# Three token tiles instead of one pass the feed-forward layer in fp32 from unsplit weights, and every later block holds one tile

## The chip, the cores and the metric

The kernel runs on one core of a Trainium2 chip. The metric is the device time of one execution in microseconds (us): the median of three runs is 649.31, the lowest 649.01, the highest 651.72. One execution was also recorded by the profiler.

## What is computed

Attention with rotary position embedding, then a feed-forward layer (FFN) on its output. The weights arrive as float64.

```python
q_rot, k_rot = (rotate(q), rotate(k))            # q, k, v: 4 x 8 heads x 576 x 64
scores = scale * np.matmul(q_rot, k_rot.transpose(0, 1, 3, 2))
scores = scores - np.max(scores, axis=-1, keepdims=True)
attn = np.exp(scores)
attn = attn / (np.sum(attn, axis=-1, keepdims=True) + 1e-09)
x = np.matmul(attn, v)                           # heads joined: x is 2304 x 512
h = x @ w_in                                     # 512 x 2048
relu6 = np.clip(h + 3.0, 0.0, 6.0)
g = h * relu6 / 6.0
out = (g @ w_out).astype(np.float32)             # 2048 x 512
```

## The kernel before, in words

The 2304 tokens are 18 tiles of 128 rows (`NT`), and tile t has 8 heads, so there are 144 attention steps. Tile 0 is done in fp32 throughout (`attention_first`, `emit_first`). The 136 steps of tiles 1 to 17 work on split numbers: an fp32 matrix is cut into a high and a low fp16 half, and a product is the sum of three fp16 products (high-high, high-low, low-high).

One fp16 attention step (`attention`) is: four matmuls for the scores S (L610; L613 where a tile belongs to two batches, as tiles 4 and 13 do), a scaling with the row maximum on VectorE (L657), the exponential on ScalarE (L659), the high half on ScalarE (L666), the low half on VectorE (L670), a DMA transposition, and 14 matmuls with V (L628). S has two buffers, which are free again after L670.

The weights are loaded in 16 pieces, 8 of w_in and 8 of w_out. Each is decoded from float64 (`decode_w`; L530, L543 or L545, L551, and L557 on VectorE), bounded (L247 or L249), and later split: `split_w_steps` makes the high half by ScalarE, GpSimd or VectorE (L292, L296, L294) and the low half by VectorE (L304, 128x1024). The split halves overwrite the unsplit weights, so a piece is split only when the tiles that need it unsplit have used it (`used_h` and `used`).

The FFN goes block by block (`BLK`). Blocks 0 to 3 hold one tile each, blocks 4 to 10 two tiles each. `ffn_h` makes x @ w_in: for each of 16 slices of 128 hidden columns it runs 4 fp32 matmuls (block 0, L893) or 12 fp16 matmuls (L906), whose moving side has 128 columns for one tile and 256 for two. `gate` makes g on ScalarE and VectorE and, for fp16 blocks, splits it into halves. `ffn_o` makes g @ w_out: per tile 16 fp32 matmuls of 512 columns (block 0, L973) or 48 fp16 ones (L977). `NF` and `NH` give how many blocks go in fp32. For an fp16 block `emit_x` divides the attention output by the row sums, splits it and transposes it by DMA.

The order of the work is not written by hand. The class `Emission` plays the program through with assumed durations and a table of priorities (`CFG`), and the instructions are recorded in the order in which this play starts them; on the chip each engine then runs its own list in that order, waiting where it must. Rules in the play: attention step i is let in by `attn_ready` (among other things: no more than `lead` = 32 steps ahead of the FFN's units, and from step 16 on only when the first w_out piece is split). `keep_clock` puts idle matmuls (L1031, result unused) into TensorE's gaps until tile 2's attention is done.

Of the kernel before, what the change touches and what calls it, by code (L numbers as in the profile page):

```python
# [185 lines left out]
def attention_ffn(ctx: ExitStack, tc, q, k, v, w_in, w_out, rope, ident, out):  # L186
# [610 lines left out]
    def emit_first():  # L797
# [19 lines left out]
        free("av")  # L817
        x_done.add(0)

    def emit_x(t):  # L820
# [20 lines left out]
        yield from scaled("xh", 512, x16[:, 0:512], x)
        e = yield "Xxl", {"P": 1.16, "d": 0.68}
        ENG[e].tensor_tensor(out=x16[:, 512:1024], in0=x, in1=x16[:, 0:512], op=ALU.subtract)  # L843
        if n == 0:
            yield "C", lambda: ((j < 3 or (j - 3) in h_done)
                                and (j % 3 == 0 or min([wdone["i"]] + used_h) >= 5 + j % 3))
            nn = 128 * len(BLK[j])
            xT_t[j] = xT_mem[j % 3][:, 0:8 * nn].rearrange("p (c n) -> p c n", c=8)
# [11 lines left out]
    def scales(j):  # L860

        for sums, kind, x in ((osc, "i", GAM * 2.0 ** -28), (out_sc, "o", 2.0 ** -16 / 6.0)):
            yield "C", lambda: kind in p2w
# [8 lines left out]

    def ffn_h(js):

        for j, ts in ((j, BLK[j]) for j in js):
# [4 lines left out]
            xT = xT_t[j]  # L880
            for u in range(4 * len(ts)):
                yield "R", "g"
                pooled = g_free.pop()
                yield "R", "h"
                h = psum.tile([128, nm, N], F32, tag="h", bufs=2, name="h")
                for i in range(nm):
                    m = u * nm + i
# [10 lines left out]
                    yield "C", lambda: wdone["i"] >= p  # L898
                    n = 0
                    for c in range(4):  # L900
                        if j < len(BLK) - 1:
                            yield "E", 0.67 / nm
                        elif c == 0:
                            yield "E", 4 * 0.65 / nm
# [233 lines left out]
```

## Time and profile before

| | |
|---|---|
| median of the runs | 649.31 us |
| profiled execution, first to last instruction | 647.6 us |
| TensorE matmuls busy | 579.7 us (90%) |
| VectorE busy | 457.2 us (71%) |
| ScalarE busy | 386.1 us (60%) |
| GpSimd busy | 309.1 us (48%) |

The profile's page gives busy times for the whole execution, but the stages differ. In the first 64 us weights are loaded and decoded and tile 0 is in attention; from some 200 us on TensorE is busy nearly throughout; between them lies a stretch in which TensorE has gaps and VectorE hardly any. The span of the profiled execution is 1.7 us under the median of the runs. Busy time of matmuls includes a modelled tail of some 0.16 us after each group, in which the next group already runs.

### The profile page before, as it was taken

The page shows a single profiled execution, that of the slowest core. Times are in us where ns is not written, and L with a number is a line of the kernel's source. Part 1 is how long each engine was busy: PE and PEld are TensorE (multiplying, and loading weights), DVE is VectorE, ACT ScalarE, POOL GpSimd, SP SyncE. Part 2 cuts the span into 40 slices and gives each one's busy share as a digit, 9 for nine tenths or more (in the row PEclk, how much of TensorE's full clock was granted, in tenths as well). Part 3 has the DMA queues.
Part 4 walks back from the last instruction along what each step waited for, and adds up shares of the span by engine and source line. Part 5 has one row for each costly group of instructions (what it writes and reads, how often), then busy time and mean ns, then how long its engine had stood idle before and what let it go on. Part 6 is the DMA issues. An engine that isn't in the chain of part 4 may idle for free.

```text
span 647.6 us, 15265 instructions
## 1 busy us (share of the span) xinstructions
PE 579.7 (90%) x6024; PEld 421.3 (65%) x6024; DVE 457.2 (71%) x860; ACT 386.1 (60%) x716; POOL 309.1 (48%) x347
## 2 busy tenths in 40 slices
PE   2488889478889999998998999999999999999997
PEld 1367755366666776675675767776677677667756
DVE  6999979999976896588697787775777656312430
ACT  4875998745855676577576756665567556322111
POOL 3573545597425596545399452562445425133000
PEclk9989889989989999999999999999999999999999
DMA  9995494986969988999998999778699775410000
GB/s 309 319 321 138 143 262 96 198 139 108 199 129 165 212 158 142 182 157 187 213 151 138 171 225 184 122 151 143 114 161 178 111 142 98 84 33 17 1 17 33
DMA packets 252439, 97.98 MB, mean 151 GB/s; under 512 B 235856, under 2 KB 236240, under 8 KB 252368
## 3 DMA queue, kind: packets, MB, share of 16 engines
q1 hardware_dynamic: 252368, 97.01, 73.4%
q8 instruction: 47, 0.77, 0.5%
q14 instruction: 24, 0.20, 0.1%
HBM read 31.97 MB, written 4.72 MB: 57 GB/s over the span
## 4 chain that ended last, share of the span: by engine, by line
PE 62%; DVE 12%; POOL 9%; DMA 8%; issue 6%; ACT 3%; SPq 0%; DVEq 0%; POOLq 0%; ACTq 0%
PE o L977 22%; PE h L906 20%; DMA PT<-P 7%; PE av L628 7%; PE S L610 6%; POOL ropeA L279 2%; PE o L973 2%; DVE P L670 2%; POOL kst L284 2%; DVE S L657 2%; POOL kst L282 2%; PE S L699 1%; PE S L613 1%; PE h L893 1%; DVE tg L930 1%
## 5 line engine op out<-in xcount | busy, mean ns | idle before, releaser
L906 PEld LDWEIGHTS <-wi_st 128*128 128x128 f16 x1920 | 164.8, 99 | 52.6 <-issue 3.0
L977 PE MATMUL o<-wo_st,g 128*128 128x512 f16 (+1 forms) x738 | 184.2, 367 | 3.7 <-ACT wo_st L1001 1.6
L906 PE MATMUL h<-wi_st 128*128 128x256 f16 (+1 forms) x1344 | 160.1, 259 | 0.8 <-DVE tg L930 0.7
L659 ACT ACTIVATE S<-S,mx 128x576 f32<-128x576 f32 x136 | 97.0, 713 | 101.9 <-DVE S L657 100.2
L657 DVE TENSOR_SCALAR_CACHE_REDUCE S<-S,sig 128x576 f32<-128x576 f32 x136 | 109.6, 819 | 33.2 <-PE S L610 26.4
L670 DVE SCALAR_TENSOR_TENSOR P<-S,P 128x576 f16<-128x576 f32 x136 | 100.9, 752 | 31.9 <-ACT P L666 31.5
L977 PEld LDWEIGHTS <-g 128*128 128x128 f16 x738 | 69.1, 98 | 44.4 <-POOL g L941 6.2
L296 POOL TENSOR_SCALAR g<-tg 128x512 f16<-128x512 f32 x37 | 23.6, 638 | 153.8 <-DVE tg L930 144.2
L930 DVE SCALAR_TENSOR_TENSOR tg<-tg,h 128x512 f32<-128x512 f32 x68 | 46.4, 683 | 70.8 <-ACT tg L923 70.8
L923 ACT ACTIVATE tg<-h,g,block_sc 128x512 f32<-128x512 f32 x68 | 52.7, 775 | 71.8 <-PE h L906 70.7
L628 PEld LDWEIGHTS <-PT 128*128 128x128 f16 (+1 forms) x2128 | 72.8, 102 | 34.7 <-DMA PT<-P 17.7
L610 PE MATMUL S<-kT,qT 128*128 128x288 f16 x480 | 77.0, 289 | 14.0 <-DVE P L670 13.9
L666 ACT ACTIVATE P<-S 128x576 f16<-128x576 f32 x135 | 85.5, 647 | 1.8
L628 PE MATMUL av<-vA,PT 128*128 128x64 f16 (+1 forms) x1520 | 63.8, 196 | 13.3 <-DMA PT<-P 12.3
L906 PE MATMUL h<-xTa,wi_st 128*128 128x256 f16 (+1 forms) x576 | 68.4, 255 | 0.0
L610 PEld LDWEIGHTS <-qT 128*128 128x128 f16 x480 | 44.1, 99 | 33.4 <-DVE P L670 13.8
L941 POOL TENSOR_TENSOR g<-tg,g 128x512 f16<-128x512 f32 x51 | 59.2, 1161 | 8.2 <-ACT g L292 5.3
L628 PE MATMUL av<-vB,PT 128*128 128x64 f16 (+1 forms) x608 | 38.9, 195 | 0.0
L977 PE MATMUL o<-wo_st 128*128 128x512 f16 (+1 forms) x126 | 32.7, 369 | 0.6 <-POOL wo_st L941 0.6
L279 POOL TENSOR_TENSOR ropeA<-kst,rope_sb 128x512 f32<-128x512 f32 (+1 forms) x16 | 20.9, 1307 | 13.3 <-DMA kst<-in_k 12.6
L843 POOL TENSOR_TENSOR x<-x,x 128x512 f16<-128x512 f32 x15 | 18.2, 1215 | 18.0 <-ACT x L292 18.0
L659 ACT ACTIVATION_READ_ACCUMULATOR S<-S,mx 128x1 f32 x136 | 26.6, 195 | 0.0
(157 smaller groups left out, 794.6 us busy)
## 6 DMA issues: line engine op xcount, KB each, us to landing
raw<-in_w_in SPq DMA_DIRECT2D x16, 512.0 KB, 7.4
raw<-in_w_out SPq DMA_DIRECT2D x16, 512.0 KB, 4.7
qraw<-in_q SPq DMA_DIRECT2D x18, 256.0 KB, 3.3
kst<-in_k SPq DMA_DIRECT2D x16, 256.0 KB, 4.0
out<-wo_st SPq DMA_DIRECT2D x16, 256.0 KB, 2.5
vst<-in_v SPq DMA_DIRECT2D x15, 256.0 KB, 4.8
PT<-P SPq DMA_TRANSPOSE x136, 3.4
vB<-vA SPq DMA_DIRECT2D x8, 256.0 KB, 3.6
```

Of the source, the lines that this page charges most:

```text
L279: ENG[e].tensor_tensor(out=v4(ta), in0=x4[:, :, ::-1, :], in1=sinb.to_broadcast([n, 8, 2, 32]), op=ALU.mult)
L610: PE.matmul(out=S[:, j, 0:288], lhsT=qT_t[t][:, o, h, :], rhs=kT_t[b0][:, h, ks], **st)
L628: PE.matmul(out=av[r0:r1, h, :], lhsT=PT[:, blk, r0:r1], rhs=rhs, start=(n == 0), stop=(n == len(terms) - 1))
L657: DVE.tensor_scalar(out=E, in0=E, scalar1=sig_t[t], scalar2=3.0e38, op0=ALU.mult, op1=ALU.min, accum_out=mx)
L659: ACT.activation(out=E, in_=E, func=ACTF.Exp, scale=-1.0, bias=mx, accum_out=sum_t[t][:, h:h + 1])
L666: ACT.activation(out=hi, in_=E, func=ACTF.Copy, scale=ES)
L670: DVE.scalar_tensor_tensor(out=lo, in0=E, scalar=ES, in1=hi, op0=ALU.mult, op1=ALU.subtract)
L906: PE.matmul(out=h[:, i, :], lhsT=wi_h(p, wl)[:, 256 * c + f0:256 * c + f0 + 128], rhs=xT[:, 4 * xl + c, :], start=(n == 0), stop=(n == 11))
L923: ACT.activation(out=tg, in_=hf, func=ACTF.Relu, scale=osc[j], bias=g3)
L930: DVE.scalar_tensor_tensor(out=whole if j < NF else tg, in0=tg, scalar=6.0 * GAM, in1=hf, op0=ALU.min, op1=ALU.mult)
L941: ENG[e].tensor_tensor(out=gf[:, 1], in0=tg, in1=gf[:, 0], op=ALU.subtract)
L977: PE.matmul(out=os[n][0][:, to], lhsT=g[:, gl, mm % nm, 128 * n:128 * n + 128], rhs=wo_h(mm, wl)[:, cs], start=(mm == 0 and gl == 0 and wl ...
```

## The change

`NF` and `NH` go from 1 to 3: tiles 0, 1 and 2 go through both products in fp32 with unsplit weights, and the pieces are split only behind tile 2. Every block holds one tile, so there are 18 blocks, and all fp16 matmuls of the first product have 128 moving columns. For tiles 1 and 2 a new `emit_x32` divides, transposes x on TensorE in fp32 and copies it. The first three tiles' attention no longer waits for w_out's splits. The first product's generator gets a priority of its own (`CFG["h"]`, 6.0), and the other numbers of `CFG` are new: `lead` goes from 32 to 18, `kvs` from 1 to 0 (the second batch's K and V are started when all 16 pieces are decoded, instead of when w_out's third piece is split), `vpos` from 0 to 3.

```diff
-BLK = [[0]] + [[t] for t in range(1, 4)] + [[t, t + 1] for t in range(4, NT, 2)]
+BLK = [[t] for t in range(NT)]
...
-NF = 1
-NH = 1
+NF = 3
+NH = 3
...
         return ((i < 16 or t - 2 in x_done) and t in qT_t and all(b in kT_t for b in BAT[t])
                 and (i == 0 or i - 1 in started) and units_done[0] >= i - CFG["lead"]
-                and (i < 16 or wdone["o"] >= CFG["a16"]))
+                and (t < NF or wdone["o"] >= CFG["a16"]))
...
-    xT_mem = [xT_a, wi16[:, 8], wi16[:, 9]]
+    slots = [xT_a[:, 1024 * a:1024 * a + 1024] for a in (NF % 2, 1 - NF % 2)] + \
+        [wi16[:, r, 1024 * a:1024 * a + 1024] for r in (8, 9) for a in (0, 1)]
...
+    def emit_x32(t):
...
+        DVE.tensor_tensor(out=x.rearrange("p (h d) -> p h d", d=64), in0=av_t[t],
+                          in1=r[:, :, None].to_broadcast([128, 8, 64]), op=ALU.mult)
...
+        yield "C", lambda: t < 2 or t - 2 in h_done
+        xT = xT_a.bitcast(F32)[:, 512 * (t % 2):512 * (t % 2) + 512].rearrange("p (c n) -> p c n", c=4)
+        yield from transposed(x, 128, [xT])
...
+            yield "C", lambda: j - 2 in h_done if m < 2 else j - 6 in h_done if m > 5 else wdone["i"] >= 6 + (m > 3)
+            xT_t[j] = slots[m % 6].rearrange("p (c n) -> p c n", c=8)
...
-                yield "C", lambda: wdone["o"] > 0 if j else (0, 0) in g_t
+                yield "C", lambda: wdone["o"] > 0 if j >= NF else (j, 0) in g_t
...
-        spawn([ffn_h(range(len(BLK) - 1)), ffn_o()], 6)
+        spawn(ffn_h(range(len(BLK) - 1)), CFG["h"])
+        spawn(ffn_o(), 6)
```

Counted over the whole program, the fp32 matmuls of the first product go from 64 to 192 and of the second from 16 to 48; the fp16 ones of the first from 576 with 128 columns and 1344 with 256 to 2880 with 128; the full-width fp16 ones of the second from 768 to 672; 8 fp32 transpositions on TensorE are new; and the idle matmuls go from 116 to 40.

Two places in VectorE's list and one in TensorE's show the move. First VectorE before, at the 14th to 16th fp16 step (tile 2): S is a step's scores (L657), P its halves (L670), wo_st and wi_st the weights, k the second batch's keys.

```order
L657 TENSOR_SCALAR S,mx<-S,sig 128x2x288 x2
L304 SCALAR_TENSOR_TENSOR wo_st<-wo_st,wso 128x2x512
L670 SCALAR_TENSOR_TENSOR P_1296<-S,P_1296 128x576
L670 SCALAR_TENSOR_TENSOR P_1300<-S,P_1300 128x576
L304 SCALAR_TENSOR_TENSOR wi_st<-wi_st,wsi 128x1024
L304 SCALAR_TENSOR_TENSOR k_1334<-kst,ks,k_1334 128x8x64
L221 TENSOR_SCALAR qp_1349<-qam 128x1
L223 TENSOR_SCALAR qp_1349<-qp_1349 128x1
L353 RECIPROCAL qs<-qp_1349 128x1
L657 TENSOR_SCALAR S,mx<-S,sig 128x2x288
L304 SCALAR_TENSOR_TENSOR wo_st<-wo_st,wso 128x2x512
L304 SCALAR_TENSOR_TENSOR wi_st<-wi_st,wsi 128x1024
```

The same three steps of the changed kernel; L958 is the gate of an fp32 tile.

```order
L657 TENSOR_SCALAR S,mx<-S,sig 128x2x288 x2
L958 SCALAR_TENSOR_TENSOR g<-tg,h 128x512
L670 SCALAR_TENSOR_TENSOR P_1238<-S,P_1238 128x576
L670 SCALAR_TENSOR_TENSOR P_1251<-S,P_1251 128x576
L657 TENSOR_SCALAR S,mx<-S,sig 128x2x288
L304 SCALAR_TENSOR_TENSOR k_1297<-kst,ks,k_1297 128x8x64
L247 TENSOR_REDUCE qam<-qraw 128x1
```

The four weight splits between the steps are gone from here. They come back later, as at the 24th step of the changed kernel (tile 3):

```order
L670 SCALAR_TENSOR_TENSOR P_1568<-S,P_1568 128x576
L304 SCALAR_TENSOR_TENSOR k_1574<-kst,ks,k_1574 64x8x64
L657 TENSOR_SCALAR S,mx<-S,sig 128x2x288
L304 SCALAR_TENSOR_TENSOR wi_st<-wi_st,wsi 128x1024
L670 SCALAR_TENSOR_TENSOR P_1587<-S,P_1587 128x576
L304 SCALAR_TENSOR_TENSOR wi_st<-wi_st,wsi 128x1024
L958 SCALAR_TENSOR_TENSOR g<-tg,h 128x512
```

Ahead of the 29th scaling stand six of w_in's eight low halves and one of w_out's; before, all sixteen.

TensorE before, behind the scores of the 11th fp16 step; 17 pairs of weight load and idle matmul stand there:

```order
L610 LDWEIGHTS qT
L610 MATMUL S<-kT_168,qT 128x288
L1031 LDWEIGHTS id_sb
L1031 MATMUL idle<-id_sb 128x256
...
L610 LDWEIGHTS qT
```

TensorE of the changed kernel, behind the scores of the 15th step (L1001 and L923 are the second and first product in fp32):

```order
L610 LDWEIGHTS qT
L610 MATMUL S<-kT_143,qT 128x288
L1001 MATMUL o<-wo_st,g 128x512
L923 MATMUL h<-xTa,wi_st 128x128 x4
L1001 MATMUL o<-wo_st,g 128x512
L923 MATMUL h<-xTa,wi_st 128x128 x4
L628 LDWEIGHTS PT
L628 MATMUL av<-vA_134,PT 128x64
```

Where idle matmuls stood, fp32 products of the first tiles now alternate with the steps. Ahead of the 29th fp16 step the list before has tile 0's FFN, 252 fp16 matmuls of the first product and 48 of the second; the changed list has 184 of the 192 fp32 matmuls of the first product, 41 of the 48 of the second, and no fp16 one.

## Rows read from the trace of the kernel before

**Rows 1.** The profile's page: span, and the weight loads of L906
```profile
span 647.6 us, 15265 instructions
...
L906 PEld LDWEIGHTS <-wi_st 128*128 128x128 f16 x1920 | 164.8, 99 | 52.6 <-issue 3.0
```

**Rows 2.** Stages: start:end and length, each engine's busy us, granted clock, DMA share, GB/s
```profile
0.00:64.00 64.00, 37.28 (x220) 30.50 (x221) 54.64 (x77) 40.63 (x70) 32.47 (x35) 0.97 0.89 272
64.00:115.00 51.00, 44.56 (x333) 32.17 (x331) 45.05 (x71) 44.73 (x66) 25.31 (x18) 0.93 0.61 168
115.00:147.00 32.00, 19.79 (x236) 15.44 (x237) 31.15 (x53) 19.49 (x35) 24.93 (x23) 0.89 0.88 163
147.00:194.50 47.50, 40.16 (x531) 30.09 (x527) 40.03 (x75) 30.41 (x56) 21.58 (x30) 0.96 0.84 150
194.50:300.00 105.50, 99.86 (x1313) 73.33 (x1311) 81.31 (x175) 69.77 (x139) 64.63 (x74) 1.00 0.94 172
```

**Rows 3.** TensorE by line, 64 to 194.5 us: busy, mean ns, idle before and releaser
```profile
L610 PE MATMUL S<-kT,qT 128*128 128x288 f16 x88 | 15.2, 300 | 10.4 <-DVE P L670 10.4
...
L1031 PE MATMUL idle<-id_sb 128*128 128x256 f16 x99 | 14.5, 287 | 0.3 <-ACT x L811 0.3
...
L628 PE MATMUL av<-vA,PT 128*128 128x64 f16 x240 | 12.2, 203 | 9.3 <-DMA PT<-P 9.3
```

**Rows 4.** VectorE by line, 64 to 194.5 us, same columns
```profile
L657 DVE TENSOR_SCALAR_CACHE_REDUCE S<-S,sig 128x576 f32<-128x576 f32 x28 | 22.6, 816 | 6.4 <-PE S L610 3.6 <-PE S L613 2.6
...
L304 DVE SCALAR_TENSOR_TENSOR wi_st<-wi_st,wsi 128x1024 f16<-128x1024 f32 x8 | 12.2, 1541 | 0.0
L304 DVE SCALAR_TENSOR_TENSOR wo_st<-wo_st,wso 128x1024 f16<-128x1024 f32 x8 | 10.6, 1324 | 0.0
...
L294 DVE TENSOR_SCALAR wi_st<-wi_st,wsi 128x1024 f16<-128x1024 f32 x3 | 4.2, 1440 | 0.0
...
L930 DVE SCALAR_TENSOR_TENSOR tg<-tg,h 128x512 f32<-128x512 f32 x5 | 3.4, 674 | 0.0
...
L247 DVE TENSOR_REDUCE wamo<-wo_st 128x1 f32<-128x1024 f32 x2 | 2.4, 1213 | 0.0
```

**Rows 5.** VectorE by line, 0 to 64 us
```profile
L294 DVE TENSOR_SCALAR vA<-wo_st,vs 128x512 f16<-128x512 f32 x5 | 3.4, 696 | 0.0
...
L294 DVE TENSOR_SCALAR wo_st<-kst,ks 128x512 f16<-128x512 f32 x3 | 2.4, 842 | 0.0
L304 DVE SCALAR_TENSOR_TENSOR wo_st<-kst,ks,wo_st 128x512 f16<-128x512 f32 x3 | 2.1, 740 | 0.0
...
L279 DVE TENSOR_TENSOR wo_st<-qraw,rope_sb 128x512 f32<-128x512 f32 x1 | 0.7, 679 | 0.0
```

**Rows 6.** VectorE in order of time at 194.6 us: start, duration, instruction
```profile
194.61 0.81 DVE L657 TENSOR_SCALAR_CACHE_REDUCE S<-S,sig 128x576 f32<-128x576 f32 x1
```

**Rows 7.** TensorE in order of time, single groups: start, duration with tail, instructions
```profile
93.26 1.02 PE L973 MATMUL o<-wo_st,g 128*128 128x512 f32 x2
94.12 1.05 PE L893 MATMUL h<-xTa,wi_st 128*128 128x128 f32 x8
...
103.83 1.37 PE L1031 MATMUL idle<-id_sb 128*128 128x256 f16 x11
...
152.76 1.34 PE L906 MATMUL h<-wi_st 128*128 128x128 f16 x21
153.93 0.81 PE L977 MATMUL o<-wo_st,g 128*128 128x512 f16 x3
...
578.16 2.78 PE L906 MATMUL h<-xTa,wi_st 128*128 128x256 f16 x24
...
622.01 7.29 PE L977 MATMUL o<-wo_st,g 128*128 128x512 f16 x33
```

**Rows 8.** ScalarE by line, 64 to 194.5 us: w_out's high halves
```profile
L292 ACT ACTIVATE wo_st<-wo_st,wso 128x1024 f16<-128x1024 f32 x8 | 9.2, 1145 | 1.8 <-DVE wso L239 1.5 <-DVE wo_st L304 0.3
```

**Rows 9.** The last gate, in order of time
```profile
622.21 0.78 ACT L923 ACTIVATE tg<-h,g,block_sc 128x512 f32<-128x512 f32 x1 [3.14 <-PE h L906]
...
624.21 0.69 DVE L941 TENSOR_TENSOR g<-tg,g 128x512 f16<-128x512 f32 x1
```

More of the change, by code (lines that the diff above doesn't have):

```diff
@@ L31 @@
 NR1 = 2
-NF = 1
-NH = 1
+NF = 3
+NH = 3
 NQ = 1
 NPT = 4
-CFG = {'a0': -0.441, 'a1': 2.342, 'a2': 2.34, 'k1': -0.119, 'kv': 4.706, 'q1': -2.636, 'q': 0.81, 'wi': 0.692, 'wo': 0.308, 'gate': 1.71, 'x': -3.065, 'lead': 32, 'lat': 0.008, 'dma': 1.996, 'back': 2.043, 'a16': 1, 'v0': -0.014, 'wb': -0.814, 'si': 7.622, 'so': 7.383, 'bias': [{'loD': -0.61, 'elD': 18.62, 'glD': -2.57, 'ehD': 4.31, 'ghD': 4.27, 'ropeD': 7.56, 'xhD': 10.68, 'xlD': -0.65, 'hiP': 0.06, 'ehP': -4.01, 'ghP': 3.58, 'xhP': 0.03, 'lowP': -3.42, 'sgP': 4.11, 'hiD': -0.4, 'wboD': 0.46, 'qbD': 0.95, 'biD': 1.37}, {'loD': -0.71, 'elD': 6.88, 'glD': 1.23, 'ehD': 0.32, 'ghD': 3.03, 'ropeD': 3.19, 'xhD': 13.25, 'xlD': -6.92, 'hiP': 0.41, 'ehP': 3.42, 'ghP': 1.83, 'xhP': -0.58, 'lowP': -7.4, 'sgP': -3.17, 'hiD': 14.08, 'wboD': 0.58, 'qbD': -0.3, 'biD': -2.3}, {'loD': -7.67, 'elD': -3.51, 'glD': 10.89, 'ehD': 3.14, 'ghD': 3.74, 'ropeD': 0.06, 'xhD': 10.21, 'xlD': 6.87, 'hiP': 4.14, 'ehP': -11.5, 'ghP': -0.2, 'xhP': 4.05, 'lowP': -3.13, 'sgP': -2.69, 'hiD': 5.89, 'wboD': 12.87, 'qbD': 3.38, 'biD': -0.89}], 'kvs': 1, 'vpos': 0, 'q0': 'D', 'ch': -0.724, 'ks': -6.026}
+CFG = {'a0': 3.98, 'a1': 0.549, 'a2': 2.562, 'k1': -10.533, 'kv': 5.894, 'q1': -9.614, 'q': -8.909, 'wi': 8.539, 'wo': 2.379, 'gate': 1.556, 'x': 1.92, 'lead': 18, 'lat': 0.008, 'dma': 1.996, 'back': 2.84, 'a16': -1, 'v0': 7.138, 'wb': 0.14, 'si': 29.208, 'so': 27.458, 'bias': [{'loD': -25.29, 'elD': 30.44, 'glD': -23.41, 'ehD': 5.44, 'ghD': 6.41, 'ropeD': 3.15, 'xhD': -3.18, 'xlD': 10.16, 'hiP': -5.16, 'ehP': 3.22, 'ghP': 32.47, 'xhP': -22.16, 'lowP': -1.63, 'sgP': 22.22, 'hiD': 1.33, 'wboD': -0.83, 'qbD': 17.49, 'biD': 3.68}, {'loD': -7.37, 'elD': -0.52, 'glD': 6.57, 'ehD': 4.32, 'ghD': 9.87, 'ropeD': 6.32, 'xhD': 36.87, 'xlD': 5.25, 'hiP': 9.51, 'ehP': 31.33, 'ghP': 2.47, 'xhP': -0.59, 'lowP': 1.65, 'sgP': 7.24, 'hiD': 11.6, 'wboD': -2.86, 'qbD': -0.87, 'biD': 12.89}, {'loD': -6.82, 'elD': -12.4, 'glD': 4.99, 'ehD': 13.5, 'ghD': -8.39, 'ropeD': 1.95, 'xhD': 7.66, 'xlD': 0.87, 'hiP': 10.6, 'ehP': -13.67, 'ghP': -15.77, 'xhP': 12.65, 'lowP': 19.72, 'sgP': -17.01, 'hiD': 13.19, 'wboD': 4.83, 'qbD': 9.06, 'biD': 5.18}], 'kvs': 0, 'vpos': 3, 'q0': 'P', 'ch': -6.436, 'ks': -9.625, 'h': 6.0}
 class Emission:
@@ L818, in emit_first @@
         x_done.add(0)
+    def emit_x32(t):
+        yield "R", "x"
+        yield "C", lambda: BAT[t][0] in p2v
+        yield "D", 1.05
+        r = col("rsum", 8, 2)
+        DVE.tensor_scalar(out=r, in0=sum_t.pop(t), scalar1=EPS, scalar2=ES, op0=ALU.add, op1=ALU.mult)
+        DVE.reciprocal(out=r, in_=r)
+        x = left.tile([128, 512], F32, tag="x", name="x")
+        DVE.tensor_tensor(out=x.rearrange("p (h d) -> p h d", d=64), in0=av_t[t],
+                          in1=r[:, :, None].to_broadcast([128, 8, 64]), op=ALU.mult)
+        yield "N", 0.0
+        free("av")
+        yield "C", lambda: t < 2 or t - 2 in h_done
+        xT = xT_a.bitcast(F32)[:, 512 * (t % 2):512 * (t % 2) + 512].rearrange("p (c n) -> p c n", c=4)
+        yield from transposed(x, 128, [xT])
+        free("x")
+        if t == 1:
+            yield "P", 0.5
+            for n, (sums, by) in enumerate(((osc, GAM * 2.0 ** -14), (out_sc, 2.0 ** -14 / (6.0 * GAM)))):
+                sc = block_sc[:, n:n + 1]
+                POOL.tensor_scalar(out=sc, in0=p2v[0], scalar1=by, scalar2=None, op0=ALU.mult)
+                sums.update({x: sc for x in range(1, NF)})
+        yield "N", 0.0
+        xT_t[t] = xT
+        x_done.add(t)
     def emit_x(t):
+        if t < NF:
+            yield from emit_x32(t)
+            return
         j, n = BLK_OF[t]
@@ L844, in emit_x @@
         if n == 0:
[L845 to L848, printed above, removed]
+            m = j - NF
+            yield "C", lambda: j - 2 in h_done if m < 2 else j - 6 in h_done if m > 5 else wdone["i"] >= 6 + (m > 3)
+            xT_t[j] = slots[m % 6].rearrange("p (c n) -> p c n", c=8)
         yield "Z", 0.9
@@ L853, in emit_x @@
         x_done.add(t)
-    block_sc = col("block_sc", 2 * len(BLK))
+    block_sc = col("block_sc", 2 * (1 + len(BLK) - NF))
     g_t, units_done, G = {}, [0], []
@@ L864, in scales @@
             yield "P", 0.5
-            sc = block_sc[:, 2 * j + (kind == "o"):2 * j + (kind == "o") + 1]
+            at = 2 * (1 + j - NF) + (kind == "o")
+            sc = block_sc[:, at:at + 1]
             POOL.tensor_tensor(out=sc, in0=fsc[j], in1=p2w["i"], op=ALU.mult)
@@ L897, in ffn_h @@
                         continue
-                    yield "C", lambda: wdone["i"] >= p
+                    if wdone["i"] < p:
+                        yield "C", lambda: wdone["i"] >= p
+                    yield "E", 4 * 0.655 / nm
                     n = 0
                     for c in range(4):
[L901 to L904, printed above, removed]
                         for wl, xl in ((0, 0), (0, 1), (1, 0)):
```

## Prediction, made before the changed kernel ran

> **What bounds the kernel now.** I read the table of stages first [rows 2]. From 194.5 to 300 us TensorE is busy 99.86 of 105.5 us at the full clock, and it stays so to the end: there the time is TensorE's work. Before 194.5 us it is not. From 64 to 194.5 us TensorE is busy 104.5 of 130.5 us (44.56 + 19.79 + 40.16), and 99 of its matmuls are idle ones [rows 3]. In the middle stage, 115 to 147 us, it is busy 19.79 of 32 us while VectorE is busy 31.15 of 32 [rows 2]: VectorE sets the pace. The grouped lines say how the wait looks: scores wait 10.4 us in all for VectorE's low half of P, which frees S [rows 3], because VectorE splits weights between the steps [rows 4]. So the question is what the change takes from VectorE before about 195 us, and what it adds to TensorE everywhere.
>
> **TensorE's added work.** Pitches, with the modelled tail of about 0.16 us taken off: one fp32 matmul of the second product 0.86 us (94.12 - 93.26; the trace shows two records for one), four fp32 matmuls of the first product 0.89 (8 records, 1.05 - 0.16), so 0.222 each; an fp16 matmul of 128 columns 0.056 (153.93 - 152.76 over 21), of 256 columns 0.109 (2.62 over 24), of 512 columns 0.216 (7.13 over 33), an idle one 0.109 (1.21 over 11) [rows 7].
> Two tiles to fp32 cost 128 x 0.222 - 384 x 0.056 = 28.4 - 21.5 = +6.9 us in the first product and 32 x 0.86 - 96 x 0.216 = 27.5 - 20.7 = +6.8 in the second. Fourteen tiles one by one instead of in pairs cost 2688 x 0.056 - 1344 x 0.109 = 150.5 - 146.5 = +4.0; the gates are as many (four units a tile) either way. Eight fp32 transpositions at the same 0.222 cost 1.8, and 76 idle matmuls fewer give back 8.3.
>
> The sum is +11.2 us. Nothing hides it while TensorE is the bound, so the change gains only if it closes more than 11 us of gaps.
>
> **What VectorE is relieved of.** The 29th fp16 step's scaling is a mark that both lists have. Before, 28 stand ahead of it [rows 4] and it starts at 194.6 us [rows 6], with VectorE busy 170.9 us until then (sum of rows 2). In the changed list, ahead of the mark: 7 low halves of w_out fewer (7 x 1.324 = 9.3), 2 of w_in (3.1), 3 high halves of w_in (3 x 1.44 = 4.3) [rows 4], 5 high halves of V (3.5), 3 of K (2.5), one rope of q, three operations of 0.68 (2.0) [rows 5]: -24.7. More: 3 bounds of w_out (3.6), 2 gates (11 instead of 9, 1.4) [rows 4], 2 low halves of K (1.5) [rows 5]: +6.5. Smaller ones on both sides I count as even. Net -18.2. What left goes partly to GpSimd and ScalarE, which are busy 72 and 95 of the 130.5 us [rows 2], so they cover it; if GpSimd were late with V's halves, tile 1's first products would wait, a few us at most. If VectorE keeps its 23.7 us of idle time, the mark comes at 194.6 - 18.2 = 176.4 us.
>
> **What is late next.** By the mark TensorE must have done more: against before, 120 fp32 matmuls of the first product (26.6), 25 of the second (21.5) and 8 transpositions (1.8) come in, 252 fp16 ones of the first (14.1), 48 of the second (10.4) and all but some ten of the idle ones (9.7) go out: +15.7 on the busy 104.5. From this I take off what the lower clock cost: the granted clock was 0.93, 0.89 and 0.96 in the three stages [rows 2], and in each a part ran at 1.2 instead of 2.4 GHz after gaps; over their lengths that is 3.6 + 3.5 + 1.9 = 9.0 us, some 80% of it under work, 7 us. If the gaps are filled, about 113 us of work remain, from the first fp16 scaling on, which comes 6.5 us earlier than 64 us (all of rows 5 lies ahead of it), at 57.5. With idle time as from 194.5 to 300 us (5.3%) that ends at 177; with that of 147 to 194.5 us (15.5%, both engines at 84%) at 191. VectorE alone says 176. Two engines of which each is needed 90% of the time, in fixed lists, do not interlock without loss: I take 182, nearer the low end because at 147 to 194.5 TensorE also lacked work that is now there.
>
> **After the mark.** Before, 647.6 - 194.6 = 453.0 us remain. The attention left is the same (107 steps). The FFN left is smaller: before 324 x 0.056 + 1344 x 0.109 + 720 x 0.216 + 96 x 0.109 = 330.6 us, changed 8 x 0.222 + 2880 x 0.056 + 7 x 0.86 + 672 x 0.216 + 96 x 0.109 = 324.7: -5.9. The splits that moved behind the mark (9 low halves, 12 us of VectorE) fall where VectorE is busy 77% [rows 2] and hide, except that tile 3's second product must wait for w_out's halves one by one; I put 2 us on it (bounds 0 and 22, below). At the end one tile's gate has less to hide behind. Its last chain takes 2.9 us (622.01 to 624.90) [rows 7, 9]; in the changed list 21 of the first 36 half-width matmuls of the last tile stand ahead of its last first-product group, 15 behind it (15 x 0.109 = 1.6), so TensorE waits 1.3 us there.
>
> Sum: 182 + 453.0 - 5.9 + 2 + 1.3 = 632.4 us of span. The runs' median lies 1.7 above the profiled span (649.31 - 647.6) [rows 1], so 634.1; I say 634.
>
> At 128 columns 21 pairs of weight load and matmul in a row run at 56 ns, and 33 matmuls of 512 columns at 216 ns [rows 7]; the sum above goes by these. A rule speaks against the change: "TensorE: Matmul & The Clock Gate", section Back-to-back issue gap, of the Trainium skill, says that in a stream of such pairs the pitch is set by both operations, about 81 ns at 128 columns and 131 at 512. This trace disagrees at both ends. By that rule the 2880 matmuls would cost an estimated 72 us more than by the trace, and the time would be 706.
>
> **Rivals.** First, the mark does not move. Chunks of 0.86 to 0.89 us [rows 7] stand between a step's matmuls where idle ones of 0.109 or nothing stood; a step that is ready waits for the chunk, and 29 steps with two such waits, each up to 0.9 us, could eat the 18 us. For it speaks that S has two buffers only; against it, that VectorE has other work while it waits. Then 194.6 + 453.0 - 5.9 + 3.3 + 1.7 = 647.
>
> Second, and slower, late splits. w_out's piece may be split only behind tile 2's fp32 use, and the pieces go one after another: 1.145 us on ScalarE [rows 8] and 1.324 on VectorE [rows 4], with a scaling of 0.816 queued between them 3.3 each, 26 us for eight. Tile 3's second product cannot pass them in TensorE's list, and all later output stands behind it. TensorE lives on first products meanwhile; where these have run out, all but some 4 us (a dozen scores at their share of rows 3) lie open, 22 us instead of my 2, and the time is 634.1 + 20 = 654. It decides from about 17 us of stall on, since 15 is what the rest gains and 2 are in the sum. Against it: the list puts tile 3's and 4's first products there, 10.8 us a tile.
>
> Third, weight loads bind at 128 columns. One load takes 99 ns [rows 1] and must overlap its neighbours to fit into 56; beside 256 columns, 109 ns covered it. Without overlap 2880 x 0.043 = 124 us come on top, 758; with half of that 696. Against it stand the 21 in a row at 56 ns.
>
> That the order does not do what the change says is ruled out by the lists: splits and idle matmuls are gone from the places shown.
>
> **How the numbers follow.** About 0.5% (3.2 us) is what a measurement can tell from no change. Forecast 72%, from 625 (VectorE alone sets the mark, 176.4, and nothing waits behind it: 176.4 + 453.0 - 5.9 + 1.7) to 643 (the mark at 191), all faster. First rival 14%, two thirds of it within 0.5%, the rest a little faster. Second 12%, a quarter of it within 0.5%, the rest slower. Third 2%, slower. Together 0.76 faster, 0.13 same, 0.11 slower. The range, 624 to 650, takes in the first rival and the near part of the second; the forecast's own range is 625 to 643.
>
> **What would show it.** The 29th L657 near 182 us; TensorE's idle time between 58 and 182 under 20 us at a clock near 1.00 there; 56 ns for the 128-column matmuls throughout; some 325 us of FFN left behind the mark. I am wrong if the mark stays at 190 or later (rival 1), if TensorE stands between the last fp32 and the first tens of fp16 second products (rival 2), or if L934's pitch is above 60 ns (rival 3).

## The result, and the profile after

The changed kernel takes 631.56 us (median of four runs, 626.69 to 636.6) against 649.16 (648.95 to 651.72) for the kernel before: ratio 0.9689, 95% interval 0.9633 to 0.9744. Predicted were 634.0 and a range of 624 to 650. The total is right; two of its terms are each wrong by more than 10 us, in opposite directions.

The ratio leaves out the longest of the four runs (636.6 us), which counts as slow because it lies over 1.5% above the fastest; that run is also the one in the profile (span 634.5). So the numbers of a second profile of the same kernel (experiment e6, span 630.8) stand beside the main readings.

The stages of [rows 2], after. Columns: start:end and length, busy us of TensorE, its weight loads, VectorE, ScalarE and GpSimd, granted clock, DMA share, GB/s:

```profile
0.00:64.00 64.00, 36.79 (x224) 29.85 (x224) 50.74 (x67) 44.22 (x71) 44.95 (x45) 0.97 0.93 271
64.00:115.00 51.00, 38.68 (x292) 29.59 (x293) 33.03 (x55) 32.22 (x51) 20.85 (x17) 0.83 0.71 171
115.00:147.00 32.00, 31.18 (x263) 22.75 (x263) 28.62 (x60) 17.18 (x33) 23.46 (x23) 1.00 0.81 148
147.00:194.50 47.50, 44.99 (x400) 33.18 (x400) 38.36 (x75) 32.70 (x59) 13.30 (x19) 0.96 0.80 157
194.50:300.00 105.50, 104.82 (x1479) 78.80 (x1478) 88.18 (x169) 69.54 (x129) 63.05 (x71) 1.00 0.83 157
```

From 115 us on TensorE is busy nearly throughout (31.18 of 32 us where it had 19.79). The stage from 64 to 115 us has become worse: TensorE busy 38.68 us (40.83 in e6) instead of 44.56, VectorE 33.03 (33.25) instead of 45.05, and the clock granted at 0.83 (0.83) instead of 0.93. Neither engine is full there.

TensorE by line, 64 to 194.5 us, against [rows 3] (busy, mean ns, idle time before and who ended it):

```profile
L923 PE MATMUL h<-xTa,wi_st 128*128 128x128 f32 x363 | 49.9, 286 | 0.0
L1001 PE MATMUL o<-wo_st,g 128*128 128x512 f32 x80 | 43.4, 629 | 0.0
L610 PE MATMUL S<-kT,qT 128*128 128x288 f16 x94 | 15.7, 296 | 5.6 <-DMA qT<-q 5.1 <-DVE P L670 0.5
L628 PE MATMUL av<-vA,PT 128*128 128x64 f16 x240 | 11.9, 201 | 12.8 <-DMA PT<-P 12.8
```

The wait of the scores for VectorE's P has gone (10.4 to 0.5 us), as forecast. Waits for two DMA transpositions stand in its place: 12.8 us for P (9.7 in e6, and 9.3 before) and 5.1 for q (2.0 in e6, none before). VectorE now waits for TensorE's scores, 21.4 us (19.0 in e6), which [rows 4] showed with 3.6:

```profile
L657 DVE TENSOR_SCALAR_CACHE_REDUCE S<-S,sig 128x576 f32<-128x576 f32 x28 | 22.7, 819 | 21.4 <-PE S L610 21.4
```

And the mark, the 29th fp16 scaling, comes no earlier than in [rows 6] (in e6 1.8 us earlier); it stands second here:

```profile
196.62 0.75 DVE L670 SCALAR_TENSOR_TENSOR P<-S,P 128x576 f16<-128x576 f32 x1
197.29 0.82 DVE L657 TENSOR_SCALAR_CACHE_REDUCE S<-S,sig 128x576 f32<-128x576 f32 x1
```

Added up over each trace, in us (the mark to the end is span less mark; TensorE's idle time is counted up to its last matmul, 3.2 to 3.3 us ahead of the end):

| | before | changed | changed again (e6) |
|---|---|---|---|
| span | 647.6 | 634.5 | 630.8 |
| first fp16 scaling | 64.1 | 66.9 | 66.3 |
| mark | 194.6 | 197.3 | 192.8 |
| VectorE busy until the mark | 171.0 | 153.5 | 155.3 |
| from the first scaling to the mark | 130.5 | 130.4 | 126.5 |
| TensorE busy in that stretch | 104.5 | 116.8 | 116.1 |
| granted clock in that stretch | 0.93 | 0.93 | 0.93 |
| from the mark to the end | 453.0 | 437.2 | 438.0 |
| TensorE idle behind the mark | 12.0 | 3.7 | 4.3 |
| TensorE idle, whole span | 64.7 | 46.5 | 42.7 |

So by the mark all of the gain (in e6 all but 1.8 us) lies behind it, where the prediction had put 2.6 us (453.0 to 450.4), and none ahead of it, where it had put 12.6. The mark is a place in VectorE's list, though. TensorE's gaps ahead of it did shrink, from 52.7 us to 42.8 (38.4 in e6), but TensorE was busy 12.5 us longer there, so that the mark did not move.

**Why the mark did not move.** SyncE issues the transpositions and the weight loads from one list. Its records in order of time, 55 to 100 us (start, duration of a group of one line with its waits inside, instruction):

```profile
55.41 0.81 SPq L508 DMA_DIRECT2D raw<-in_w_out  x2
...
57.50 3.49 SPq L366 DMA_TRANSPOSE qT<-q  x1
61.03 0.57 SPq L313 DMA_DIRECT2D qraw<-in_q  x1
74.02 0.81 SPq L508 DMA_DIRECT2D raw<-in_w_out  x2
74.94 2.16 SPq L676 DMA_TRANSPOSE PT<-P  x1
77.20 0.90 SPq L508 DMA_DIRECT2D raw<-in_w_out  x1
78.21 1.40 SPq L676 DMA_TRANSPOSE PT<-P  x1
79.66 13.96 SPq L508 DMA_DIRECT2D raw<-in_w_out  x5
93.74 2.15 SPq L676 DMA_TRANSPOSE PT<-P  x1
95.94 2.84 SPq L364 DMA_TRANSPOSE qT<-q  x1
98.89 1.32 SPq L676 DMA_TRANSPOSE PT<-P  x1
```

First, q. Before the first fp16 scores both transpositions of q must land (L364, L366). The second stands behind two loads of w_out (L508), which wait until 55.41 us, and is issued at 57.50 (57.51 in e6). In the list before, it stood ahead of these loads:

```profile
49.20 2.33 SPq L366 DMA_TRANSPOSE qT<-q  x1
```

Second, P. Two of the halves of P that the transpositions move were ready on VectorE at these times:

```profile
79.95 0.74 DVE L670 SCALAR_TENSOR_TENSOR P<-S,P 128x576 f16<-128x576 f32 x1
...
81.93 0.74 DVE L670 SCALAR_TENSOR_TENSOR P<-S,P 128x576 f16<-128x576 f32 x1
```

They are complete at 80.7 and 82.7 us; their transpositions are issued at 93.74 and 98.89, 13 and 16 us later, because five loads of w_out (L508) stand ahead of them, and these wait for raw buffers that ScalarE's decoding frees late. The summed waits of SyncE's list say the same, 40 to 125 us (waiter, releaser: us, times, longest):

```profile
SPq L508 <- ACT tw L551: 23.6, 3, 12.4
SPq L508 <- ACT wo_st L551: 14.3, 2, 7.3
```

What TensorE made of it (the wait in brackets):

```profile
66.10 1.14 PE L610 MATMUL S<-kT,qT 128*128 128x288 f16 x4 [5.09 <-DMA qT<-q]
...
80.49 0.47 PE L628 MATMUL av<-vA,PT 128*128 128x64 f16 x10 [2.82 <-DMA PT<-P]
...
84.04 0.72 PE L628 MATMUL av<-vA,PT 128*128 128x64 f16 x10 [1.31 <-DMA PT<-P]
...
84.78 3.57 PE L923 MATMUL h<-xTa,wi_st 128*128 128x128 f32 x16
88.18 0.65 PE L610 MATMUL S<-kT,qT 128*128 128x288 f16 x4
...
100.01 0.47 PE L628 MATMUL av<-vA,PT 128*128 128x64 f16 x10 [3.19 <-DMA PT<-P]
```

During or right behind such waits the clock stood at 1.2 GHz for 17 us in all between 64 and 112 us, and four fp32 matmuls of the first product (eight records) took 1.81 us there (at 80.91) instead of [rows 7]'s 1.05. The scores at 88.18 stood behind eight more of them, which took 3.57 us at that clock, and VectorE waited for these scores:

```profile
88.87 0.83 DVE L657 TENSOR_SCALAR_CACHE_REDUCE S<-S,sig 128x576 f32<-128x576 f32 x1 [5.61 <-PE S L610]
```

So VectorE's 21.4 us are in part TensorE's waits and in part fp32 work that stood ahead of the scores. e6 shows the same: L508 waits of 22.9 and 13.0 us, a granted clock of 0.82 from 58 to 115 us.

### The profile page after: what moved, and what is told of

It reads as the page before. It is cut to its first block, busy times and chain, and to the rows that moved or that the text cites. A ratio compares the mean times of both kernels' runs of the same rounds, so it can differ in the third digit from the quotient of the medians.

```text
span 634.5 us, 17495 instructions
## 1 busy us (share of the span) xinstructions
PE 584.6 (92%) x7140; PEld 445.7 (70%) x7140; DVE 448.6 (71%) x837; ACT 376.5 (59%) x693; POOL 323.5 (51%) x387
## 4 chain that ended last, share of the span: by engine, by line
PE 75%; DMA 9%; DVE 6%; POOL 4%; issue 3%; ACT 2%; SPq 1%; DVEq 0%; POOLq 0%; ACTq 0%
PE h L934 23%; PE o L1005 23%; PE av L628 8%; PE S L610 8%; DMA PT<-P 6%; PE o L1001 5%; PE h L923 4%; DMA qT<-q 1%; PE S L613 1%; DMA qraw<-in_q 1%; POOL wo_st L296 1%; DVE S L657 1%; POOL vA L296 1%; DVE P L670 1%; DVE wo_st L304 1%
## 5 line engine op out<-in xcount | busy, mean ns | idle before, releaser
L934 PEld LDWEIGHTS <-wi_st 128*128 128x128 f16 x2880 | 177.1, 98 | 38.2 <-issue 3.1
L1005 PE MATMUL o<-wo_st,g 128*128 128x512 f16 (+1 forms) x612 | 154.4, 367 | 0.8 <-DVE g L294 0.4
L657 DVE TENSOR_SCALAR_CACHE_REDUCE S<-S,sig 128x576 f32<-128x576 f32 x136 | 110.4, 820 | 50.1 <-PE S L610 39.8
L670 DVE SCALAR_TENSOR_TENSOR P<-S,P 128x576 f16<-128x576 f32 x136 | 101.1, 752 | 32.4 <-ACT P L666 32.1
L934 PE MATMUL h<-wi_st 128*128 128x128 f16 x1728 | 119.4, 219 | 0.0
L951 ACT ACTIVATE tg<-h,g,block_sc 128x512 f32<-128x512 f32 x68 | 52.7, 775 | 69.2 <-PE h L934 61.0
L934 PE MATMUL h<-xTa,wi_st 128*128 128x128 f16 x1152 | 79.5, 219 | 0.0
L958 DVE SCALAR_TENSOR_TENSOR tg<-tg,h 128x512 f32<-128x512 f32 x60 | 41.0, 684 | 48.3 <-ACT tg L951 48.0
L1005 PEld LDWEIGHTS <-g 128*128 128x128 f16 x612 | 52.4, 98 | 26.2 <-DVE g L294 0.7
L923 PEld LDWEIGHTS h<-xTa,wi_st 128*128 128x128 f32 x384 | 50.6, 200 | 13.4 <-issue 12.7
L923 PE MATMUL h<-xTa,wi_st 128*128 128x128 f32 x384 | 52.8, 286 | 0.0
L1001 PE MATMUL o<-wo_st,g 128*128 128x512 f32 x96 | 51.9, 626 | 0.0
L1005 PE MATMUL o<-wo_st 128*128 128x512 f16 (+1 forms) x156 | 38.8, 363 | 0.6 <-ACT wo_st L1045 0.6
```

The lines of the kernel that those rows point to most:

```text
L657: DVE.tensor_scalar(out=E, in0=E, scalar1=sig_t[t], scalar2=3.0e38, op0=ALU.mult, op1=ALU.min, accum_out=mx)
L670: DVE.scalar_tensor_tensor(out=lo, in0=E, scalar=ES, in1=hi, op0=ALU.mult, op1=ALU.subtract)
L951: ACT.activation(out=tg, in_=hf, func=ACTF.Relu, scale=osc[j], bias=g3)
L1001: PE.matmul(out=os[n][0], lhsT=g[:, mm % nm, 128 * n:128 * n + 128], rhs=wo_st[:, mm + 2], start=(mm == 0), stop=(mm == 15))
L1005: PE.matmul(out=os[n][0][:, to], lhsT=g[:, gl, mm % nm, 128 * n:128 * n + 128], rhs=wo_h(mm, wl)[:, cs], start=(mm == 0 and gl == 0 and wl ...
```

## Experiments

Each was run beside the kernel before on the same chip. Theory Q: the loads in SyncE's list hold the mark back. G: blocks of one tile close the gaps behind the mark. V: it is all VectorE's relief. N: the new numbers of the play do it. One edit can reorder everything, since the play is worked out anew for each kernel except e5.

**e5: w_out's loads from ScalarE's list.** TensorE's, VectorE's and GpSimd's lists stay as they are.

```diff
-                SP.dma_start(out=dst, in_=src)
+                (SP if kind == "i" else ACT).dma_start(out=dst, in_=src)
```

> The changed kernel with w_out's loads issued from ScalarE's queue instead of SP's; every other list stays as it is. Theory Q (between 58 and 115 us the transpositions of P and q stand in SP's queue behind loads that wait for a free buffer): TensorE's idle time there falls from 15.3 us to 6 or less, the 29th scaling comes at 190 or before instead of 197, and the time falls by 5 to 10 us, to 622 to 627. Rival D (the DMA engines are simply full there, or ScalarE's decoding is late): idle time and mark stay, 630 to 634.

**e6: the changed kernel once more**, on the same chip as e5.

> The changed kernel once more, beside the others on the same chip: 627 to 636, and a profile in which the waits of the first profile between 58 and 115 us (15.3 us idle) are seen again if they belong to the lists, and not if they belong to that one execution.

e5 took 625.03 us (620.62 to 626.99; ratio 0.9604, 0.9532 to 0.9676), e6 632.35 (627.57 to 633.67; 0.9723, 0.9662 to 0.9785): 7.3 us apart, with runs that do not overlap. From 58 to 115 us, e6 first:

```profile
58.00:115.00 57.00, 45.66 (x333) 35.90 (x334) 37.59 (x59) 38.67 (x62) 26.07 (x25) 0.82 0.73 178
```

```profile
58.00:115.00 57.00, 45.90 (x369) 34.61 (x369) 43.76 (x70) 40.15 (x63) 27.10 (x23) 0.92 0.70 154
```

TensorE is busy as long, but with 369 instead of 333 records, at 0.92 instead of 0.82 of the clock. The mark comes at 186.7 instead of 192.8, and from there to the end it takes as long as in e6 (437.8 and 438.0 us). Of these 6.1 us, 5.0 are there by the first scaling (61.3 instead of 66.3): q's second transposition is issued 12 us earlier, and no score waits for q.

```profile
45.44 2.58 SPq L366 DMA_TRANSPOSE qT<-q  x1
```

Only the place of sixteen DMA issues differs, so the 7.3 us are shown to be its doing, and the place of q's transposition is the part that can be followed. For P's transpositions Q is not shown: no load stands ahead of them in SyncE's list any more, yet TensorE's waits for them from 64 to 194.5 us stay (e6 first, then e5).

```profile
L628 PE MATMUL av<-vA,PT 128*128 128x64 f16 x240 | 11.8, 200 | 9.7 <-DMA PT<-P 9.7
```

```profile
L628 PE MATMUL av<-vA,PT 128*128 128x64 f16 (+1 forms) x320 | 13.1, 196 | 10.1 <-DMA PT<-P 10.1
```

One wait of 7.01 us in e5, at 80.22, was for a transposition issued at 68.07, among loads that ScalarE issued. It took 12.1 us to land (DMA, count, us from issue to landing):

```profile
PT<-P SPq DMA_TRANSPOSE x1, 12.1
```

From the first scaling to the mark e5 takes 125.4 us instead of 126.5: TensorE is busy 4.9 us less, at a clock of 0.97 instead of 0.93, and idle 3.8 us more. The Trainium skill, "Trainium Kernel Development and Optimization", section Key Constraints, says that issuing DMAs from several engines saves only the sequencer's issue time; here the other list also ended waits of 36 us (22.9 + 13.0) that stood ahead of transpositions. TensorE's idle time from 58 to 115 us hardly fell, from 11.3 to 11.1 us, and not to 6 or less: in this rival D was right, in the mark and the time Q.

**e8: a pause ahead of each w_out load**, so that the play puts them later in SyncE's list.

```diff
+            if kind == "o":
+                yield "U", 4.0
```

> The changed kernel, but the play issues each of w_out's loads 4 us later, so that they stand further back in SP's list; the lists are played anew. Theory Q: less idle time between 58 and 115 us (under 9), 623 to 629. Rival D: no less idle time there, 630 or more.

618.48 us (616.38 to 620.25), ratio 0.9522 (0.9469 to 0.9574): the fastest of all, 31 us under the kernel before and 14 under the changed one of the same chip (e6), and below Q's range too. The mark comes at 177.2 us. SyncE's list and VectorE's P, same columns as above (the edit moves line numbers by two):

```profile
66.51 3.17 SPq L510 DMA_DIRECT2D raw<-in_w_out  x4
72.03 3.07 SPq L678 DMA_TRANSPOSE PT<-P  x2
```

```profile
71.22 0.75 DVE L672 SCALAR_TENSOR_TENSOR P<-S,P 128x576 f16<-128x576 f32 x1
```

```profile
L659 DVE TENSOR_SCALAR_CACHE_REDUCE S<-S,sig 128x576 f32<-128x576 f32 x33 | 26.6, 817 | 3.5 <-PE S L612 3.4
```

P is ready at 71.97 us and its transposition is issued at 72.03. No matmul waits for P's or q's transposition between 58 and 115 us, and VectorE's wait for scores is 3.4 us where it was 21.4. The loads still wait 17.2 us in SyncE's list. The first scaling is nearly as late as in e6 (65.8 and 66.3 us); the gain lies between it and the mark, 111.4 us, in which TensorE is busy 106.3 us at a clock of 1.00.

**e10: another play, without a purpose**, as a control for e8: `CFG["lat"]` 0.020 instead of 0.008.

> A control: the changed kernel, with the play's assumed latency between engines 0.020 instead of 0.008 us and nothing else, so that its lists come out differently at many places without a purpose. It says how much a new play of the same rules moves the time by itself. If theory Q is right in saying that the place of the loads gave the pause its 13 us, this one stays near the changed kernel, 626 to 640 us, with waits of over 10 us at the loads in SyncE's list. The rival, that the gain of the pause was luck of the play, allows 618 as easily, with the loads' waits as long as before.

643.84 us (641.6 to 644.97; 0.9897, 0.9861 to 0.9934), outside both. The waits at L508 are there (20.9 and 16.0 us) and the mark comes at 201.5, as Q says, but 5.2 us of gaps also came back between 300 and 450 us (0.5 in the changed kernel, 5.3 before). A change of 12 ns in one assumption thus moves the time by 12 us. So e8's 14 us cannot be put on the loads alone; the 7.3 of e5 can, since there only the place of the loads differs.

**e11: a pause of 7 us.**

> The changed kernel with a pause of 7 instead of 4 us ahead of each w_out load. Theory Q: the loads no longer wait in SyncE's list, but eight pauses of 7 us put the last piece some 24 us later than with 4, so tile 3's products wait or the play fills the time otherwise: 618 to 628 us, with waits at the loads under 5 us. Theory D (ScalarE's decoding and the transfers are simply full at 58 to 115 us) expects that later is better still: 612 to 617.

625.41 us (625.23 to 626.66; 0.9622, 0.9595 to 0.9649), as Q expected, and later was not better, against D. The loads wait 5.9 us in all (longest 4.6), a little over the 5 expected, the clock from 58 to 115 us is 1.00, and TensorE idles 6.6 us there. The mark still comes only at 192.4: more of VectorE's work (161.6 us) stands ahead of it in this list.

**e9: the same pause in the kernel before.**

> The kernel before with the 4 us pause ahead of each w_out load, its order worked out anew. Theory Q (w_out's loads that wait in SyncE's list for raw buffers hold up the transpositions behind them) sees such waits in the kernel before too, 15.4 and 11.0 us, but there VectorE sets the pace up to the mark (171 of 194.6 us busy), so little should come of it: 643 to 651 us, and the mark at 188 to 196. The rival, that the pause helps any play because loads and decodes spread out, gives what it gave the changed kernel, 12 to 14 us: about 636.

669.04 us (668.57 to 671.44; 1.0287, 1.0254 to 1.032). Both missed, and the mark came at 208.9. TensorE's idle time behind 195 us rose from 12.0 to 30.3. The pause as such speeds nothing up; why this play is so much worse was not followed further.

**e1: blocks of one tile alone**: one fp32 tile, the old numbers and `"h": 6.0`, and the old rule that step 16 waits for w_out's first split.

```diff
-NF = 3
-NH = 3
+NF = 1
+NH = 1
```

> Only tile 0 in fp32, but every block one tile, with the numbers of the order of before. Theory V (the gain comes from VectorE being relieved of the weight splits early): nothing is relieved, TensorE's work is 4.0 us more by the wider count of 128-column matmuls, so about 649 + 4 = 653, and gaps between 195 and 450 us as before (about 11 us idle). Rival G (one-tile blocks give TensorE work in the gaps after the mark): those gaps nearly close, 649 + 4 - 10 = 643.

639.23 us (634.67 to 642.01; 0.9812, 0.975 to 0.9875). The mark is late (201.1, VectorE busy 173.8 until then), yet from there to the end it takes 436.2 us instead of 453.0. Of these 16.8 us, 6.5 are gaps of TensorE that have closed (12.0 to 5.5), as G has it; the rest is work that this play puts ahead of its later mark. V, with 653, fails.

**e2: three fp32 tiles, later blocks of two tiles**, the new numbers with their lead of 18; x has room for three blocks again, which is six tiles as in the changed kernel.

```diff
-BLK = [[t] for t in range(NT)]
+BLK = [[t] for t in range(4)] + [[t, t + 1] for t in range(4, NT, 2)]
```

> Tiles 0, 1 and 2 in fp32 and the new numbers, but from tile 4 on two tiles a block. Theory V: as the changed kernel less the 4.0 us, 631.6 - 4 = 627 to 628. Rival G: the gaps between 195 and 450 us come back (10 us), 637 to 638.

687.36 us (686.44 to 698.02; 1.0556, 1.0516 to 1.0597). Both missed: pairs wait for the attention of two tiles, and with lead 18 it does not run far enough ahead. TensorE idles 46.8 us behind the mark; its first products wait 16.0 us there for x, and not at all with lead 32 (e7).

**e7: e2 with lead 32**, and **e12: the changed kernel with lead 32**, to part the two.

> Three tiles in fp32, pairs from tile 4 on, the new numbers with lead at 32 instead of 18, so that attention may run as far ahead of pairs as before. Theory G (blocks of one tile close the gaps after the mark): 637 to 642, with 8 to 12 us idle between 195 and 450 us. Rival V: 626 to 630, as the changed kernel less the 4 us of the wider matmul count.

> The changed kernel with lead 32 instead of 18, the fourth corner beside pairs with 18 (687), one tile with 18 (632) and pairs with 32 (653). Theory G (blocks of one tile close the gaps behind the mark): 627 to 637 us, idle time of TensorE from 300 us to the end under 5 us. The rival, that the shorter lead closes them: 645 to 655, with 10 us or more of idle time behind 300 us.

e7 took 653.24 us (651.68 to 662.15, ten runs; 1.0075, 1.0036 to 1.0115), e12 627.56 (626.07 to 634.25; 0.9671, 0.9607 to 0.9735). TensorE by line from 195 us to the end, pairs first, then one tile:

```profile
L610 PE MATMUL S<-kT,qT 128*128 128x288 f16 x384 | 63.7, 296 | 11.1 <-DVE P L670 10.2 <-DVE qp L221 0.6
...
L628 PE MATMUL av<-vA,PT 128*128 128x64 f16 (+1 forms) x1280 | 52.6, 196 | 10.6 <-DMA PT<-P 10.5
```

```profile
L610 PE MATMUL S<-kT,qT 128*128 128x288 f16 x384 | 60.8, 286 | 1.3 <-DVE P L670 1.2
L628 PE MATMUL av<-vA,PT 128*128 128x64 f16 (+1 forms) x1234 | 50.4, 194 | 1.0 <-DMA PT<-P 1.0
```

With the same lead and numbers, the steps' waits are 21.7 us with pairs and 2.3 with one tile. The profile of e7 is of an execution of 661.4 us, 8 above the median, so 21.7 is at the high end. The lead does not close the gaps (18 or 32: 632 and 628 with one tile); with these numbers the size of the blocks does. How much of the 25.7 us is that these numbers were not chosen for pairs stays open.

**e3: the changed kernel with the old numbers** (and `"h": 6.0`), and **e4: the kernel before with the new ones**.

> The changed kernel with the numbers of the order of before (lead 32, kvs 1, vpos 0 and the rest; the new priority at 6.0). Theory V and rival G alike: the structure carries it, 630 to 637. Rival N (the new numbers carry it): 643 or more, with gaps of over 20 us between 58 and 195 us.

> The kernel before with the new numbers of the order. Theory V and rival G: no gain, 648 to 655, since the splits still stand early in VectorE's list and blocks are pairs. Rival N: 643 or less.

670.14 us (1.0308, 1.0266 to 1.0351) and 733.17 (1.1268, 1.1219 to 1.1318). Neither theory's sizes held. N fails as a cause by itself, since the new numbers alone cost the kernel before 82 us, but it is a condition: the new structure with the old numbers is 19 us slower than the kernel before.

One column orders all profiles, the time from the mark to the end. Nine with one tile per block: 428.8 (e3) to 441.6 us (e10). Five with pairs: 453.0 (before), 460.7 (e9), 466.3 (e7), 498.6 (e2), 521.1 (e4). The mark is a place in VectorE's list, and how much of TensorE's work stands ahead of it differs between plays, so only the two groups count, not the order within them. By TensorE's idle time behind the mark the groups overlap: one tile 3.4 to 16.9 us (e10 10.7, e3 16.9, the others 8.0 or less), pairs 12.0 to 60.7. Both times that blocks were changed under the same numbers (e1 against before, e12 against e7) the smaller ones closed gaps, but one-tile blocks in a poor play can keep the gaps of before.

## Why the prediction came out right, point by point

**TensorE's added work (+11.2 us): its counts and pitches held.** TensorE's busy time rose by less, from 579.7 to 584.6 us (584.8 in e6). It also holds modelled tails, fewer where gaps have gone, and work at the lower clock, so it does not test the sum closely. The pitch at 128 columns, from groups near the end of the changed kernel:

```profile
612.63 0.83 PE L934 MATMUL h<-wi_st 128*128 128x128 f16 x12
613.30 0.81 PE L1005 MATMUL o<-wo_st,g 128*128 128x512 f16 x3
613.95 0.83 PE L934 MATMUL h<-wi_st 128*128 128x128 f16 x12
```

Twelve in 0.67 us are 56 ns, three of 512 columns in 0.65 are 217. Over all 2880 the median is 56, so the third rival is out, and the Trainium skill's rule that stands beside the sum (81 and 131 ns) does not hold here.

**VectorE's relief (18.2 us): right in size.** It was busy 153.5 us up to the mark (155.3 in e6) instead of 171.0, which is 17.5 (15.7) less.

**"VectorE alone says 176", taken as 182: this step failed.** The mark came at 197.3 us (192.8 in e6), 15.3 (10.8) late. In the step's own terms (its idle time is 182 less 57.5 and 113):

| | forecast | changed | e6 |
|---|---|---|---|
| first scaling, us | 57.5 | 66.9 | 66.3 |
| TensorE's work from there to the mark, us | 113 | 116.8 | 116.1 |
| its idle time in that stretch, us | 11.5 | 13.6 | 10.4 |

Most of it is the start, 9.4 us (8.8). The step moved the start by the 6.5 us that VectorE loses ahead of it; but the first scores waited for q's second transposition, which stood behind loads in SyncE's list. The step took every transposition for prompt and did not look at that list, although the trace of before already had L508 waiting there for 15.4 and 11.0 us. The next part, 3.8 us (3.1), is work: the step had taken 7 us off because filled gaps would bring the full clock, and the clock stayed at 0.93 over the stretch, an estimated 9 us of it (0.07 of 130.4). The idle time was near what the step allowed. P's transpositions cost TensorE 10.0 us between 58 and 115 us (7.8 in e6) against 2.5 before, but e5 does not show that the loads in the list were the reason.

In e8 the mark came at 177.2, near the 176 of VectorE alone (busy 154.0 until then), with a first scaling no earlier. So the loss that I added for two interlocking engines need not occur; but e8 is another play, and by e10 a play without a purpose moves the mark too, to 201.5.

The first rival's sign (mark at 190 or later) appeared. Its mechanism, chunks of fp32 work ahead of a step's scores, is seen at 84.78 above; how much it cost in all is not settled. In e8, with the same fp32 products between the steps, VectorE waits only 3.4 us for scores, so the chunks alone need not hold the mark back.

The signs named beforehand were half met: TensorE idled 18.6 us between 58 and 182 us (13.4 in e6; under 20 was forecast), but at a clock of 0.83 instead of 1.00 from 64 to 115.

**"Before, 453.0 us remain", gaps unchanged: the second wrong step.** The sum had 450.4 us behind the mark (453.0 - 5.9 + 2 + 1.3); measured were 437.2 (438.0 in e6). Of the 15.8 us less than before, 8.3 are idle time of TensorE that has gone (12.0 to 3.7) and 7.5 are work, near the 5.9. I had priced the one-tile blocks by their matmuls alone (+4.0) and carried the old gaps over; the waits of the scores and of P's transposition that fill these gaps shrink with the size of the blocks (e7 and e12).

**The small terms.** Late splits, 2 us: nothing of the kind, no second product waits between 182 and 300 us, so the second rival is out. The tail, 1.3 us: 0.76, in the first two rows here; the third wait was there before.

```profile
623.15 0.39 PE L1005 MATMUL o<-wo_st,g 128*128 128x256 f16 x2 [0.42 <-DVE g L294]
623.88 1.26 PE L1005 MATMUL o<-wo_st,g 128*128 128x256 f16 x10 [0.34 <-DVE g L969]
625.76 1.47 PE L1005 MATMUL o<-wo_st 128*128 128x256 f16 x12 [0.61 <-ACT wo_st L1045]
```

Together: 15.3 us late at the mark, 13.2 early behind it, so the span was 634.5 instead of 632.4. In e6 it is 10.8 late and 12.4 early. The time was right because two errors cancelled, which is luck, and the mechanism was right only in part: VectorE was relieved and TensorE's gaps ahead of the mark shrank, but a late start, work at the lower clock and the added fp32 work kept the mark where it was; the gain that shows behind it goes with the size of the blocks. Over the whole span TensorE idled 18.2 us less (22.0 in e6) and was busy 4.9 (5.1) longer. How the 17.6 us divide between the three fp32 tiles and the one-tile blocks is not settled: e1 puts 639 between 650 and 632, but its distance of 7 us from the changed kernel is less than an aimless new play moves the time (e10).

## What to carry to other kernels

When a change relieves the engine that sets the pace, read the list of the engine that issues the DMAs before booking the gain: a load that waits there for a buffer holds back every transfer behind it. Before moving the start of a stage by what one engine saves, ask what its first step waits for. A stretch that ends at a fixed mark is worth two questions, what bounds it and what its gaps are made of; gaps are not carried over when the size of the pieces changes. Where a planner orders the work, run a version with an aimless change of the plan, to know how much of a difference means nothing.

## What the runs showed of the hardware that was not expected

P's transpositions landed late between 58 and 115 us, whichever list the loads stood in. From issue to landing the changed kernel had a median of 5.6 us there (8 transpositions; 5.2 in e6), against 3.4 over the whole program and 3.4 in the same stretch before (7). With the loads in ScalarE's list (e5) it was 5.8 (8), and one took 12.1 where the longest of the changed kernel took 7.3 (7.5 in e6). So the place of the loads in SyncE's list is not the reason; with as many loads in the stretch (10) it was 3.9 in e8 and 3.4 in e11. The reason was not found. Of these views (columns: DMA, count, us), the changed kernel's stretch comes first, then its whole program, then e5's stretch:

```profile
PT<-P SPq DMA_TRANSPOSE x8, 5.6
```

```profile
PT<-P SPq DMA_TRANSPOSE x136, 3.4
```

```profile
PT<-P SPq DMA_TRANSPOSE x8, 5.8
```
